# A planner that treats the ports shared by Vector and GpSimd as a lock, with offsets found anew

## The chip, the core and the metric

The kernel runs on one core of one Trainium2 chip. The time is device microseconds for one execution. A core has five engines that each work through a queue of their own in order: TensorE (PE in the profile, with its weight loads as PEld), VectorE (DVE), ScalarE (ACT), GpSimd (POOL) and SyncE (SP, which only starts DMAs here). They meet through semaphores alone.

## The reference, cut to what matters

```python
def reference(A_u, A_log_A_real, A_A_imag, A_C_real, A_C_imag, A_log_dt, A_D_skip, B_x, B_w_r, B_w_i, gate_w):
    x = A_u                                            # 1 x 2048 x 640
    g = _sigmoid((x * gate_w).sum(-1, keepdims=True))
    a = _A_ref(x, A_log_A_real, A_A_imag, A_C_real, A_C_imag, A_log_dt, A_D_skip)
    b = _B_ref(x, B_w_r, B_w_i)
    return g * a + (1 - g) * b

# _A_ref: K[d,l] = 2 Re sum_n C[d,n] exp(A[d,n] dt[d] l)   (640 x 128 states x 2048 positions)
#         y = irfft(rfft(u, 4096) * rfft(K, 4096))[:2048] + u * D_skip, per channel d
# _B_ref: irfft2(rfft2(x) * (w_r + 1j * w_i)) over positions and channels
```

## The kernel before, in words

All transforms are matrix products with tables. The work falls into streams, which the code names by a letter:

- **P** (`phase_p`): the preparation. Small elementwise chains on DVE and POOL turn `log_A_real`, `A_imag`, `C` and `log_dt` into eight rows of parameters. `parts` splits each into a rounded half and a rest, and writes it to the DRAM tile `par_d` by a DMA that POOL starts (L305).
- **A** (`phase_a`, first half): the forward transform of u in four chunks c of channels. Stage 1 (`p_s1`, L365) and stage 2 (`p_s2`, L378) run on PE; copies to `t1` and `ut` on ACT or DVE (L412); `ut` goes to DRAM as `u_d`. Between the halves of stage 1, gate products (`p_g`, L447) use the tile `z`, which POOL makes (L424); `z` has two buffers, so a new one waits for the gate product that read an old one.
- **B** (`phase_b`): the convolution kernel K in 40 tiles t, five at a time. Five tiles of magnitudes come first (PE `p_e` L665, ACT `e` L666), from parameters `par` that a DMA of POOL loads per five tiles (L656). Then each tile: PE `p_p` (L675), ACT and DVE `q` (L677, L678), DVE `aq` (L688), ACT `sc`, `sx`, `cx` (L690 to L693), DVE `x` (L700 to L702, against `sx` and `cx` in PSUM), POOL `y` (L705 and L706), and PE `p_k` (L719).
- **E** (`phase_a`, second half): the two-dimensional filter, in nine pairs of rows. DVE and POOL make `fo` and `fg` (L511 to L519), PE transposes and transforms, DVE multiplies (`mm`, `zz`, `pm`, L562 to L572) and combines (`xx`, `qq`).
- **D** (`phase_c`, `phase_d`): the products with the transform of K, the inverse and the gated sum. DVE makes `ma`, `mb` (from PSUM), `t2` and `oe`, POOL the other half of `t2` (L842) and the sum `ot` (L911).

The code's own order is only the input of a planner at its end. `steps` turns every instruction into a step with an engine, a length and the steps that it needs; `urgency` gives each a rank from its place in the code, the length of the work behind it, and the table `LEAD`; `arrange` walks through a modelled time and gives each engine the ready step of lowest rank; `keep_order` fixes the resulting order per engine. So a number in `LEAD` moves instructions on every engine. Before the change, the model lets DVE and POOL run side by side freely; for the preparation alone it stretches their lengths (`STRETCH`).

Of the kernel before, what the change touches and what calls it, by code (L numbers as in the profile page):

```python
# [15 lines left out]
PSUM = bass.MemoryType.PSUM  # L16
NOSYNC = mybir.DependencyInfo(mybir.DependencyClass.NoSync, mybir.DependencyReason.DATA)
DRAM = bass.MemoryType.DRAM

L = 2048  # L20
D = 640
N = 128
E = 321
# [778 lines left out]
def phase_d(tc, A, T, ctx, out):  # L802
# [174 lines left out]
RIGHT = ("a_", "f_", "c_t0", "c_k", "c_c", "c_u", "c_ps0")  # L977
SBUF_BYTES, PSUM_BYTES = 212992, 16384
DRAIN = {"PE": 0.1, "DVE": 0.083, "ACT": 0.115, "POOL": 0.045, "SP": 0.0}
STRETCH = {("P", "DVE"): 1.3, ("P", "POOL"): 1.15}  # L980
TABLES = {"Exp": "exp", "Sin": "sin", "Arctan": "sin", "Ln": "ln", "Sigmoid": "sig"}


LEAD = {
# [24 lines left out]
}  # L1009


def operands(ins, side):
    return [a for a in (getattr(o, "bass_ap", None) for o in getattr(ins, side)) if a is not None]
# [5 lines left out]

def on_chip(t):  # L1020
    return hasattr(t, "tag_meta") and "DRAM" not in str(t.space)


def pool_name(tag, pools):
# [8 lines left out]
def steps(traced):  # L1033

    insts = [x for x in traced if x.opcode != "TilePoolBoundary"]
# [3 lines left out]
    reads, writes = [[] for _ in insts], [[] for _ in insts]  # L1039
# [93 lines left out]
    for k, x in enumerate(insts):  # L1133
        e, name = ENGINES[str(x.engine).split(".")[-1]], short((writes[k] + reads[k])[0])
        if e == "PE":
            key = (writes[k][0], *(() if name == "p_s1" else (operands(x, "outs")[0].offset % 512 >= 160,) if name == "p_i2" else sorted(set(reads[k]))))
            if key in open_:
                home[k] = open_[key]
                todo[home[k]].parts.append(k)
                continue  # L1140
            open_[key] = len(todo)
        s = Step()
        s.engine, s.name, s.parts, s.dma = e, name, [k], x.opcode == "DMACopy"
        tag = [info[z].tag for z in writes[k] + reads[k] if on_chip(info[z])]
        pool = of[tag[0]] if tag else ""
        s.stream = "P" if pool in ("p1", "b_c") else "A" if pool == "cst" else {"b": "B", "a": "A", "f": "E"}.get(pool[:1], "D")
        s.table = TABLES.get(str(x.func).split(".")[-1]) if x.opcode == "Activation" else None
        s.first = reads[k]
        home[k] = len(todo)
        todo.append(s)  # L1150
    opened = {}
# [8 lines left out]
    for n, s in enumerate(todo):  # L1160
        s.needs = {home[j] for k in s.parts for j in needs[k]} - {n}
        s.behind = {home[j] for k in s.parts for j in turns[k]} - s.needs - {n}
        s.length = length(s, insts) * (1 if s.dma else STRETCH.get((s.stream, s.engine), 1))
        s.late = {"s3_d": 3.6, "t3": 4.0, "us": 3.0, "t3e": 3.0}.get(s.name, 3.4 if s.engine == "POOL" else 2.3)
        s.wire = 4 * math.prod(c for _, c in operands(insts[s.parts[0]], "outs")[0].ap) / (330e3 if s.name == "s3_d" else 390e3) if s.dma else 0
        if s.table in ("exp", "sin", "sig") and s.name in ("e", "sc", "sx", "cx", "gate"):
            s.needs |= {prior} - {None}
            prior = n
# [78 lines left out]
def arrange(todo, after, rank):  # L1247

    left = [len(s.needs | s.behind) for s in todo]
    come, start = [0.0] * len(todo), [0.0] * len(todo)  # L1250
    later = {e: [] for e in ENGINES.values()}
    ready = {e: [] for e in later}
    free = dict.fromkeys(later, 0.0)
    order = {e: [] for e in later}
    wire, table, end = 0.0, None, 0.0
    for n, c in enumerate(left):
        if not c:
            heapq.heappush(later[todo[n].engine], (0.0, n))
    for _ in todo:
        t, e = min((free[e] if ready[e] else max(free[e], later[e][0][0]), e) for e in later if ready[e] or later[e])  # L1260
        while later[e] and later[e][0][0] <= t:
            n = heapq.heappop(later[e])[1]
            heapq.heappush(ready[e], (rank[n], n))
        n = heapq.heappop(ready[e])[1]
        s = todo[n]
        start[n] = t
        own = t + s.length
        if s.table and s.table != table:
            own, table = own + 1.4, s.table
        free[e] = own  # L1270
        if s.dma:
            wire = max(wire, own) + s.wire
            own = wire + s.late
        elif e in ("DVE", "POOL"):
            own += DRAIN[e]
        seen = own + 0.05 + (DRAIN[e] if e in ("PE", "ACT") else 0)
        order[e].append(n)
        end = max(end, seen)
        for j in after[n]:
            if n in todo[j].needs:  # L1280
                come[j] = max(come[j], own if todo[j].engine == e else seen)
            left[j] -= 1
            if not left[j]:
                heapq.heappush(later[todo[j].engine], (come[j], j))
    return end, order, start
# [32 lines left out]
```

## Time and profile before

| | |
|---|---|
| time, median of 3 runs | 586.72 us (582.41 to 586.8) |
| the profiled execution | 585.55 us, span 582.6 us |
| busy PE, DVE, ACT, POOL | 512.2, 457.5, 359.0, 229.8 us |
| streams P, A, B and E | about 0 to 430 us, D from there to the end |

Busy time is the time in which an engine had an instruction of the program in work. An instruction that has been issued and stands still until something that it needs is free counts as busy, so a longer duration than that of its equals is a wait that no list of waits shows.

### The profile page before, as it was taken

To read this page: it belongs to the slowest core of one execution; us is meant where nothing else is said; L and a number is where in the kernel's file an instruction comes from. 1 tells how busy PE (TensorE), PEld (TensorE's weight loads), DVE (VectorE), ACT (ScalarE), POOL (GpSimd) and SP (SyncE) were. 2 spreads that over 40 slices of the span, in tenths; PEclk is the share of its full clock that TensorE was granted. 3 is DMA by queue.
4 is the path that set the end of the run, shared out by engine and by line. 5 is a ranking of instruction groups with operands and counts; after the bars stand their busy time and mean duration, and the time that the engine had idled before them with its cause. 6 is when DMAs were issued, how large, how long until landed. Compare 5 with 4: busy or idle time off the path is not lost. (4 is left out here: it accounts for less than half of the span.)

```text
span 582.6 us, 17664 instructions
## 1 busy us (share of the span) xinstructions
PE 512.2 (88%) x7580; PEld 382.5 (66%) x7580; DVE 457.5 (79%) x780; ACT 359.0 (62%) x655; POOL 229.8 (39%) x214
## 2 busy tenths in 40 slices
PE   2799899997888987999699999899879989999954
PEld 0798578766756756676567676666768767776621
DVE  4980369979988998998999998695956757677953
ACT  0665473567677976989778899688964333322110
POOL 3195033415432444443442451351632222635450
PEclk8899799998858998999999999699999999999997
DMA  9569415464051214124212122211849797999984
GB/s 344 193 233 357 148 47 201 157 188 168 25 169 58 75 50 136 56 68 147 114 57 69 55 70 78 92 52 46 318 167 335 239 349 282 311 324 344 346 266 174
DMA packets 47333, 100.64 MB, mean 173 GB/s; under 512 B 3204, under 2 KB 32280, under 8 KB 45368
## 3 DMA queue, kind: packets, MB, share of 16 engines
q1 hardware_dynamic: 25128, 69.35, 34.4%
q10 hardware_dynamic: 19088, 19.53, 10.1%
q0 software_dynamic: 3040, 10.65, 5.5%
q8 instruction: 59, 0.97, 0.6%
q14 instruction: 18, 0.15, 0.1%
HBM read 59.70 MB, written 39.81 MB: 171 GB/s over the span
## 5 line engine op out<-in xcount | busy, mean ns | idle before, releaser
L705 POOL TENSOR_TENSOR y<-e,sc 128x512 f32<-128x512 f32 x40 | 56.0, 1399 | 112.9 <-ACT sc L690 87.8
L378 PE MATMUL p_s<-t,w 128*64 128x160 f32 x1040 | 89.2, 312 | 2.1 <-ACT ut L412 2.0
L378 PEld LDWEIGHTS p_s<-t,w 128*64 128x64 f32 x1040 | 72.4, 137 | 19.8 <-issue 10.1
L666 ACT ACTIVATE e<-p_e 128x512 f32<-128x512 f32 x120 | 67.7, 612 | 20.4 <-PE p_e L665 19.5
L665 PE MATMUL p_e<-rm,par 128*128 128x512 f32 x120 | 57.4, 521 | 9.4 <-ACT e L666 6.1
L706 POOL TENSOR_TENSOR y<-e,sc 128x512 f32<-128x512 f32 x40 | 54.5, 1362 | 19.6 <-ACT sc L691 15.7
L678 DVE SCALAR_TENSOR_TENSOR q<-q,p_p 128x512 f32<-128x512 f32 x80 | 51.8, 676 | 12.8 <-ACT q L677 12.6
L842 POOL TENSOR_TENSOR t<-mb 128x320 f32<-128x320 f32 (+1 forms) x36 | 33.9, 943 | 70.3 <-DVE mb L840 64.8
L581 PE MATMUL p_eo<-td,pmt 107*128 107x321 f32 x204 | 58.8, 435 | 0.0
L366 ACT COPY t<-p_s 128x512 f32<-128x512 f32 x40 | 25.0, 634 | 54.3 <-PE p_s L365 43.6
L719 PE MATMUL p_k<-x,y 128*32 128x64 f32 x2560 | 45.2, 224 | 8.7 <-ACT kt L727 4.7
L675 PE MATMUL p_p<-rp,par 128*128 128x512 f32 x80 | 40.4, 534 | 14.0 <-DVE q L678 13.1
L365 PE MATMUL p_s<-c,u 128*64 128x128 f32 x640 | 40.0, 281 | 12.8 <-DMA u<-in_u_l 11.2
L719 PEld LDWEIGHTS p_k<-x,y 128*32 128x32 f32 x2560 | 39.1, 112 | 17.2 <-issue 10.7
L839 DVE TENSOR_TENSOR ma<-p_s,us 128x320 f32<-128x320 f32 (+1 forms) x68 | 32.9, 484 | 20.6 <-PE p_s L378 16.8
L702 DVE TENSOR_TENSOR x<-e,cx 128x1024 f32<-128x1024 f32 x40 | 48.3, 1208 | 0.6 <-ACT cx L693 0.6
L677 ACT ACTIVATE q<-p_p 128x512 f32<-128x512 f32 x80 | 44.9, 600 | 5.2 <-PE p_p L675 4.5
L581 PEld LDWEIGHTS p_eo<-td,pmt 107*128 107x128 f32 x204 | 38.2, 189 | 14.8
L365 PEld LDWEIGHTS p_s<-c,u 128*64 128x64 f32 x640 | 36.1, 140 | 17.9 <-DMA u<-in_u_l 12.8
L665 PEld LDWEIGHTS p_e<-rm,par 128*128 128x128 f32 x120 | 22.6, 201 | 29.5 <-ACT e L666 20.9
L365 PE MATMUL p_s<-c,kt 128*64 128x128 f32 x640 | 41.3, 274 | 0.1
L860 ACT COPY s<-p_i 128x640 f32<-128x640 f32 x32 | 20.6, 696 | 33.4 <-PE p_i L858 27.4
(152 smaller groups left out, 1093.4 us busy)
## 6 DMA issues: line engine op xcount, KB each, us to landing
u_d<-ut SPq DMA_DIRECT2D x32, 320.0 KB, 3.3
s_d<-s ACTq DMA_DIRECT2D x16, 640.0 KB, 5.8
t<-s_d SPq DMA_DIRECT2D x15, 640.0 KB, 6.5
us<-u_d ACTq DMA_DIRECT2D x13, 640.0 KB, 7.3
ww<-in_w_l SPq DMA_DIRECT2D x8, 642.0 KB, 3.9
ue<-u_d SPq DMA_DIRECT2D x8, 640.0 KB, 4.5
k_d<-kt SPq DMA_DIRECT2D x4, 1280.0 KB, 5.4
kt<-k_d SPq DMA_DIRECT2D x8, 640.0 KB, 6.2
```

The source lines that it names most:

```text
L365: nc.tensor.matmul(p[64 * ri:64 * ri + 64, j, :], src(i + j), e1[ri], start=True, stop=True)
L378: ins = nc.tensor.matmul(p[64 * j:64 * j + 64, i, 160 * ri:160 * ri + 160], w2[:, x, 64 * ri:64 * ri + 64], t1[:, x // 2 if x < 32 else K0 ...
L581: P.matmul(p[:, :E], st.pmt[:DC, c, w, j, :], tv[:DC, w, c, :], start=c == 0, stop=c == 2)
L665: P.matmul(p[:, :], pars[t], rm[:, c:c + 512], start=True, stop=True)
L666: S.activation(ef[:, c:c + 512], p[:, :], AF.Exp)
L675: P.matmul(p[:, :], pars[t], rp[:, c:c + 512], start=True, stop=True)
L677: S.activation(qf[:, c:c + 512], p[:, :], AF.Copy, bias=MAGIC)
L678: V.scalar_tensor_tensor(out=qf[:, c:c + 512], in0=qf[:, c:c + 512], scalar=MAGIC, in1=p[:, :], op0=ALU.subtract, op1=ALU.subtract)
L702: V.tensor_tensor(out=x[:, 0].rearrange("p d (h j) -> p d h j", h=2), in0=e[:, :, 0:64].rearrange("p d (h j) -> p d h j", h=2), in1=cx.uns ...
L705: G.tensor_tensor(out=y[:, 1], in0=e[:, :, 64:96], in1=sc[:, 0], op=ALU.mult)
L706: G.tensor_tensor(out=y[:, 0], in0=e[:, :, 64:96], in1=sc[:, 1], op=ALU.mult)
L719: P.matmul(st.pb[32 * r:32 * r + 32, o, :], y[:, ri, 4 * qq + JR[r], :], x[:, ri, 4 * qq + JR[r], :], start=t % 2 + qq + 1 - ri == 0, stop ...
```

## The change

The planner's time gets one variable more, `port`: the time at which the ports that DVE and POOL share become free. A step needs them (`s.port`) if POOL computes it, or if DVE runs it with all inputs in SBUF and either several inputs, or one input and an output in SBUF too. A step that needs the ports starts when they are free, and holds them until its end. Each engine's ready steps are kept in two heaps, without and with need of the ports; while the ports are taken, an engine takes a step without that need where it has one, whatever the ranks. DMAs that POOL starts are left out (`not s.dma`). `STRETCH` is dropped, and `LEAD` has the same keys with other numbers. What is computed, the buffers and the loops stay the same.

```diff
-STRETCH = {("P", "DVE"): 1.3, ("P", "POOL"): 1.15}
...
-    'mix': 0.53, 'A': (373, 290), 'B': (420, 624), 'D': (473, 238), 'E': (501, 524), 'P': (-536, -1704), ('A', 'DVE', 'ut'): -117,
+    'mix': 0.14, 'A': (279, 619), 'B': (522, 1248), 'D': (4113, 2809), 'E': (944, 678), 'P': (-1263, -2074), ('A', 'DVE', 'ut'): 143,
...
+def on_sbuf(ap):
+    return not any(w in str(ap.tensor.space) for w in ("PSUM", "DRAM"))
...
-        s.first = reads[k]
+        s.port = not s.dma and (e == "POOL" or e == "DVE" and all(on_sbuf(a) for a in operands(x, "ins")) and (
+            len(operands(x, "ins")) > 1 or x.opcode != "ScalarTensorTensor" and all(on_sbuf(a) for a in operands(x, "outs"))))
...
-        s.length = length(s, insts) * (1 if s.dma else STRETCH.get((s.stream, s.engine), 1))
+        s.length = length(s, insts)
...
-    ready = {e: [] for e in later}
+    ready = {e: ([], []) for e in later}
...
-    wire, table, end = 0.0, None, 0.0
+    wire, table, end, port = 0.0, None, 0.0, 0.0
...
-            heapq.heappush(ready[e], (rank[n], n))
-        n = heapq.heappop(ready[e])[1]
+            heapq.heappush(ready[e][todo[n].port], (rank[n], n))
+        a, b = ready[e]
+        n = heapq.heappop(a if a and (not b or b[0] > a[0] or port > t) else b)[1]
         s = todo[n]
+        if s.port:
+            t = max(t, port)
...
+        if s.port:
+            port = own + (DRAIN[e] if e == "POOL" else 0)
```

Three places show what this does to the rows.

DVE, at the products (`mm`, `zz`) of the third pair of rows of E, beside which it makes `fo` and `fg` for later pairs. Before:

```order
L702 TENSOR_TENSOR x<-e,cx 128x1024
L563 TENSOR_TENSOR mm<-xx,ww 128x642
L586 SCALAR_TENSOR_TENSOR qq<-o,c_65,p_eo 128x321
L587 SCALAR_TENSOR_TENSOR qq<-o,c_65,p_eo 128x319
L511 TENSOR_TENSOR fo<-ue 128x640
L512 TENSOR_TENSOR fo<-ue 128x640
L516 TENSOR_TENSOR fg<-fo 128x2x159
L564 TENSOR_TENSOR zz<-mm 128x321
L586 SCALAR_TENSOR_TENSOR qq<-o,c_65,p_eo 128x321
L587 SCALAR_TENSOR_TENSOR qq<-o,c_65,p_eo 128x319
L517 TENSOR_TENSOR fg<-fo 128x2x159
L565 TENSOR_TENSOR zz<-mm 128x321
```

The corresponding place after the change:

```order
L701 TENSOR_TENSOR x<-e,sx 128x16x32
L702 TENSOR_TENSOR x<-e,cx 128x1024
L516 TENSOR_TENSOR fg<-fo 128x2x159
L562 TENSOR_TENSOR mm<-xx,ww 128x642
L517 TENSOR_TENSOR fg<-fo 128x2x159
L563 TENSOR_TENSOR mm<-xx,ww 128x642
L564 TENSOR_TENSOR zz<-mm 128x321
L565 TENSOR_TENSOR zz<-mm 128x321
L511 TENSOR_TENSOR fo<-ue 128x640
L512 TENSOR_TENSOR fo<-ue 128x640
L566 TENSOR_TENSOR mm<-xx,ww 128x642
L567 TENSOR_TENSOR mm<-xx,ww 128x642
```

The steps with all inputs in SBUF (`fg`, `mm`, `zz`, `fo`) now stand together, and the `qq` and `x` steps, which read PSUM, ahead of them.

PE, where the magnitudes (`p_e`) and the first phases (`p_p`) of B begin between stage 1 and stage 2 of A's third chunk. Before:

```order
L365 MATMUL p_s_869<-c_65,u 64x128 x8
L665 MATMUL p_e<-rm,par 128x512 x2
L365 MATMUL p_s_889<-c_65,u 64x128 x8
L665 MATMUL p_e<-rm,par 128x512 x2
L447 MATMUL p_g<-u,z 32x64 x20
L675 MATMUL p_p<-rp,par 128x512 x2
L365 MATMUL p_s_947<-c_65,u 64x128 x8
```

After, from the group ahead of the last gate product to the first `p_p`:

```order
L365 MATMUL p_s_1087<-c_65,u 64x128 x8
L665 MATMUL p_e<-rm,par 128x512 x2
L447 MATMUL p_g<-u,z 32x64 x20
L665 MATMUL p_e<-rm,par 128x512 x2
L378 MATMUL p_s_1131<-t_816,w_68 64x160 x4
L665 MATMUL p_e<-rm,par 128x512
L378 MATMUL p_s_1137<-t_816,w_68 64x160 x4
L665 MATMUL p_e<-rm,par 128x512 x2
L378 MATMUL p_s_1193<-t_816,w_68 64x160 x4
L675 MATMUL p_p<-rp,par 128x512
```

The first `p_p` now stands behind five more stage 1 groups (947, 982, 1013, 1077, 1087), one more gate product and three stage 2 groups. None of the 15 `p_e` ahead of it comes before group 889 any more; 13 did.

POOL, at the end of the preparation, where `parts_203` is the last pair of parameter rows to be written to `par_d`. Before:

```order
L303 CAST parts_203<-th 128x640
L305 DMA par_d<-parts_176 128x1280
L304 TENSOR_TENSOR parts_203<-th,parts_203 128x640
L424 TENSOR_TENSOR z<-c_65,gw 128x640
L305 DMA par_d<-parts_203 128x1280
L424 TENSOR_TENSOR z<-c_65,gw 128x640 x2
L656 DMA par<-par_d 128x640 x2
```

After:

```order
L305 DMA par_d<-parts_191 128x1280
L303 CAST parts_203<-th 128x640
L424 TENSOR_TENSOR z<-c_65,gw 128x640
L304 TENSOR_TENSOR parts_203<-th,parts_203 128x640
L424 TENSOR_TENSOR z<-c_65,gw 128x640
L305 DMA par_d<-parts_203 128x1280
L656 DMA par<-par_d 128x640 x2
L424 TENSOR_TENSOR z<-c_65,gw 128x640 x2
```

Two of the `z` that stood behind the last write to `par_d` now stand ahead of it, the second of them the one that before waited for a gate product of chunk 1.

More of the change, by code (lines that the diff above doesn't have):

```diff
@@ L1259, in arrange @@
     for _ in todo:
-        t, e = min((free[e] if ready[e] else max(free[e], later[e][0][0]), e) for e in later if ready[e] or later[e])
+        t, e = min((free[e] if any(ready[e]) else max(free[e], later[e][0][0]), e) for e in later if any(ready[e]) or later[e])
         while later[e] and later[e][0][0] <= t:
             n = heapq.heappop(later[e])[1]
-            heapq.heappush(ready[e], (rank[n], n))
-        n = heapq.heappop(ready[e])[1]
+            heapq.heappush(ready[e][todo[n].port], (rank[n], n))
+        a, b = ready[e]
+        n = heapq.heappop(a if a and (not b or b[0] > a[0] or port > t) else b)[1]
         s = todo[n]
+        if s.port:
+            t = max(t, port)
         start[n] = t
```

47 rows, old and new, of the table LEAD are left out of this document.

## The prediction, made before the changed kernel ran

> **What bounds the kernel now.** I read the page's busy line first, then the busy time by stretch, then the chain that ended last.
>
> ```profile
> span 582.6 us, 17664 instructions
> PE 512.2 (88%) x7580; PEld 382.5 (66%) x7580; DVE 457.5 (79%) x780; ACT 359.0 (62%) x655; POOL 229.8 (39%) x214
> ```
>
> ```profile
> 60.00:80.00 20.00, 18.32 (x195) 12.87 (x197) 6.92 (x13) 10.67 (x19) 1.26 (x1) 0.83 0.28 92
> 80.00:100.00 20.00, 20.00 (x340) 16.59 (x338) 19.80 (x37) 11.25 (x19) 9.43 (x7) 1.00 0.41 153
> 60.00:430.00 370.00, 332.73 (x4508) 247.85 (x4508) 324.64 (x501) 288.48 (x533) 144.36 (x129) 0.94 0.32 107
> 180.00:330.00 150.00, 134.00 (x1570) 98.32 (x1572) 144.19 (x213) 124.26 (x233) 62.66 (x57) 0.97 0.27 85
> 330.00:430.00 100.00, 90.19 (x1310) 66.48 (x1299) 82.15 (x127) 87.22 (x167) 42.87 (x36) 0.95 0.32 109
> 480.00:540.00 60.00, 60.00 (x1032) 42.59 (x1028) 44.11 (x99) 18.17 (x29) 28.36 (x30) 1.00 0.91 315
> ```
>
> ```profile
> 430.22 0.64 issue
> ...
> 540.21 0.74 PE p_s L378 x8
> ```
>
> The columns after the stretch are busy us of PE, PEld, DVE, ACT and POOL, then granted clock, DMA share and GB/s. From 430 to 541 us the chain is matrix work back to back (PE 60.00 of 60): that is stream D. Ahead of it, streams A, B and E share all engines. Between 180 and 330 us DVE is the limit: 144.19 of 150 us, PE 134.00. Before and after, no engine is full (330 to 430: PE 90.19, ACT 87.22, DVE 82.15), so waits between engines set the pace.
>
> Part of DVE's busy time is no work. Here are neighbours on DVE and on POOL:
>
> ```profile
> 211.80 1.15 DVE L564 TENSOR_TENSOR zz<-mm 128x321 f32<-128x321 f32 x1
> 213.79 1.47 DVE L517 TENSOR_TENSOR fg<-fo 128x318 f32<-128x318 f32 x1
> ```
>
> ```profile
> 213.64 1.27 POOL L705 TENSOR_TENSOR y<-e,sc 128x512 f32<-128x512 f32 x1
> ```
>
> The fg step (0.48 us undisturbed, as L568 below, which has nearly its size) was issued at 213.79 while POOL's y ran until 214.91, and ended at 215.26: it began when y was done. That is the lock the new planner counts.
>
> **The change, part by part.** *The clashes.* The groups of DVE in 180 to 330 us, with mean ns after the busy us, and the spread of one line:
>
> ```profile
> L688 DVE TENSOR_SCALAR aq<-q 128x1024 int32<-128x1024 int32 x17 | 18.0, 1057 | 0.0
> L572 DVE TENSOR_TENSOR pm<-zz 128x642 f32<-128x642 f32 x5 | 5.8, 1162 | 0.0
> L571 DVE TENSOR_TENSOR pm<-zz 128x642 f32<-128x642 f32 x5 | 5.2, 1042 | 0.0
> L562 DVE TENSOR_TENSOR mm<-xx,ww 128x642 f32<-128x642 f32 x5 | 4.7, 936 | 0.0
> L567 DVE TENSOR_TENSOR mm<-xx,ww 128x642 f32<-128x642 f32 x5 | 4.1, 817 | 0.0
> L564 DVE TENSOR_TENSOR zz<-mm 128x321 f32<-128x321 f32 x5 | 3.7, 736 | 0.0
> L565 DVE TENSOR_TENSOR zz<-mm 128x321 f32<-128x321 f32 x5 | 3.5, 699 | 0.0
> L569 DVE TENSOR_TENSOR zz<-mm 128x321 f32<-128x321 f32 x5 | 3.1, 615 | 0.0
> L568 DVE TENSOR_TENSOR zz<-mm 128x321 f32<-128x321 f32 x5 | 2.4, 482 | 0.0
> L517 DVE TENSOR_TENSOR fg<-fo 128x318 f32<-128x318 f32 x5 | 3.4, 675 | 0.0
> L516 DVE TENSOR_TENSOR fg<-fo 128x318 f32<-128x318 f32 x5 | 3.1, 621 | 0.0
> ```
>
> ```profile
> L688 DVE TENSOR_SCALAR aq<-q x40: 674/683/2721, 81.7 to 422.2; 128x1024 int32<-128x1024 int32 x40
> ```
>
> Undisturbed, aq takes its median 683 ns, a 128x642 step 817 (L567), a 128x321 step 482 (L568). Lost: aq 17 x 374 = 6.4 us; pm and mm 5 x (345 + 225 + 119) = 3.4; zz 5 x (254 + 217 + 133) = 3.0; fg 5 x (193 + 139) = 1.7. Together **14.5 us**, in a stretch where DVE stands idle for only 5.8. All of it could reach the end: PE with 134.00 and ACT with 124.26 of 150 have room. What the new order saves lies between 0 (it fixes rows per engine, not when engines meet) and 14.5. The DVE excerpt shows both sides: zz, fo and mm were gathered behind the x products, which read PSUM, but fg on DVE still stands next to the fg that POOL makes from the same fo. Some aq are now followed by x, others by mm or zz, just where POOL starts y. I take half: **-7.3 us**. Outside the stretch DVE waits anyway (82.15 of 100 us from 330 on), so of what clashes cost there I count **-0.5 us**.
>
> *POOL's own DMA issues* stay outside the planner's lock.
>
> ```profile
> 286.13 0.61 POOL L656 DMA_DIRECT2D par<-par_d  x1
> ```
>
> ```profile
> 286.28 2.72 DVE L688 TENSOR_SCALAR aq<-q 128x1024 int32<-128x1024 int32 x1
> ```
>
> This aq stood 2.0 us beyond its 683 ns, behind an issue and the two fg that followed. Such clashes remain; that is a reason for half and not for all. The Trainium skill, SBUF — State Buffer (section "SBUF: two separate sides"), says that DMAs issued from GpSimd need the shared pair to write descriptors, so that a two-port Vector step and such an issue exclude each other, which the row at 286.28 fits. By that rule all 8 par issues can clash again, at 0.6 us each 4.8 us as an estimate; by the plan, none.
>
> *The start of B.* The preparation feeds par_d, whose last DMA now stands on POOL behind two z more, and the second of them waits for a gate product.
>
> ```profile
> 47.97 0.59 POOL L305 DMA_DIRECT2D par_d<-parts  x1
> 50.65 1.26 POOL L424 TENSOR_TENSOR z<-c,gw 128x640 f32<-128x640 f32 x1 [0.79 <-PE p_g L447]
> ```
>
> ```profile
> 61.68 1.19 PE L665 MATMUL p_e<-rm,par 128*128 128x512 f32 x2 [1.95 <-DMA par<-par_d]
> ```
>
> If that second z ends at 51.91 again, the DMA behind it goes out 3.9 us later than at 47.97, and the first p_e could run at 65.6 instead of 61.7. What covers it is work of A: the 13 p_e that stood ahead of p_s_889 now come behind it, so PE, free from 59.7, first does four and a half stage 2 groups and five of stage 1, 4.5 x 0.57 + 5 x 0.87 = 6.9 us (prices below), until 66.6. The cover is about 1 us thick; each us by which z waits longer than that is a us on the start of B. The move has its own price. Ahead of the first p_p stand five more stage 1 groups, one gate product and three stage 2 groups.
>
> ```profile
> 434.21 0.87 PE p_s L365 x16
> 435.09 1.14 PE p_s L378 x16
> ```
>
> ```profile
> 44.49 0.77 PE L447 MATMUL p_g<-u,z 128*32 128x64 f32 x40
> 79.26 1.29 DVE L678 SCALAR_TENSOR_TENSOR q<-q,p_p 128x512 f32<-128x512 f32 x2 [1.72 <-ACT q L677]
> L412 DVE COPY t<-p_s 128x512 f32<-128x512 f32 x20 | 13.2, 682 | 5.2 <-PE p_s L365 5.1
> L412 DVE COPY ut<-p_s 128x320 f32<-128x320 f32 x38 | 17.2, 481 | 25.5 <-DMA u_d<-ut 17.8 <-PE p_s L378 7.7
> ```
>
> A row of the order with x8 is 16 matmuls here, one with x4 is 8: 5 x 0.87 + 0.77 + 3 x 0.57 = 6.8 us, so DVE's first q comes at about 86 instead of 79.3. In return DVE has 5 t and 4 ut copies behind it by then, 5 x 0.68 + 4 x 0.48 = 5.3 us that it need not do later. Its net loss is **+1.5 us**, between -1 (PE has less to fill later) and +6.8 (the early copies only fill holes).
>
> *The rest.* In D, t2 and oe swap places with a neighbour and half of the inverse products stand together; PE's 60.00 of 60 us covers that: 0, or some 1 us if an evacuation comes late. The end (last s3 store, load and p_c) keeps its order. ACT loads as many tables. Without STRETCH the preparation steps only rank differently.
>
> Sum: -7.3 - 0.5 + 1.5 = **-6.3 us**. The profiled execution took 585.55 us (span 582.6 and 2.9 around it) and would take 579.3; it lies 1.2 us under the median of the runs, 586.72, which becomes **580.4**.
>
> **PE's clock** is the term that I can't set.
>
> ```profile
> 170.00:180.00 10.00, 9.04 (x31) 6.24 (x31) 6.59 (x12) 7.21 (x14) 2.19 (x3) 0.69 0.51 171
> 370.00:380.00 10.00, 10.00 (x97) 7.53 (x97) 3.86 (x8) 3.29 (x7) 2.59 (x2) 0.62 0.23 97
> ```
>
> ```profile
> PE p_p L675 <- DVE q L678: 13.1, 10, 3.2
> ```
>
> In these stretches the granted clock is 0.69 and 0.62, PE becomes the slow one, and DVE idles for 3.4 and 6.1 us. One such drop more or fewer is worth that much. PE's longest wait for q is 3.2 us; fewer clashes on DVE should shorten such waits, and waits at new places can bring a drop of their own. The Trainium skill, TensorE: Matmul & The Clock Gate (section "Part 1: The HAM clock gate"), halves the clock after an idle window of about 3.4 us and restores it after a busy one; by that rule waits of 3.2 us alone should cause no drop, and the sum would stand as it is. The rows show drops all the same, so here the trace does not agree; they decide, and the range takes a drop either way.
>
> **Rivals.**
> *Nothing reaches the end.* The order is by modelled times and the chip's waits drift against it; clashes move to other rows, as aq followed by mm. For: an order made without the lock already met only where the rows above show it, so there is chance in it. Against: DVE is full for 150 us. Then -0 + 1.5: about 588, and with a little saved 585.
> *All of it.* No clash stays in 180 to 330, and a steadier PE sees one clock drop fewer: 586.7 - 14.5 - 0.5 + 1.5 = 573, and 567 to 571 with that drop.
> *Slower, by the late start of B.* DVE lies two thirds idle before its first q (6.92 of 20 us); if that wait grows by all of 6.8 us because the copies moved ahead would have fitted into holes, and no clash is saved, the end comes at 586.7 + 6.8 = 593.5. It decides where savings stay under 1 us. For: between the first q and 180 us DVE has some holes (6.59 of 10 from 170 on). Against: 80 to 100 us has next to none (19.80 of 20).
>
> **How the numbers follow.** The forecast (577 to 584) has 0.38, no effect (584 to 592) 0.26, all of it (under 577) 0.18, slower (over 592.6) 0.18. One per cent, 5.9 us, is about what a measurement here tells from no change. Below 580.9 lie all of the third case and 0.26 of the forecast's own range: faster 0.44; same 0.12 + 0.26 = 0.38; slower 0.18. The range 570 to 593 leaves out the deepest savings with a clock drop fewer and the worst of the late start.
>
> **What would show it.** Clashes: between 180 and 330 us mean aq near 0.87 us instead of 1.06, pm near 0.96 instead of 1.10. Bound: DVE near 448 us in total, PE's share of the span higher. Start: first q near 86 us, par landing before PE asks for it. D: about 152 us from its start to the end, as now. I am wrong if aq stays over 1.0, if the first q comes after 90, or if the count of stretches with a halved clock changes by two.

## The result, and the profile after

The changed kernel takes **579.66 us** (median of 8 runs, 577.0 to 581.85), the kernel before on the same chips 585.41 us (8 runs, 582.41 to 588.19). The ratio is **0.9894**, with a 95% interval of 0.9859 to 0.9928. The forecast was 580.4. The profiled execution took 580.48 us. Ratios are of means, and runs over 1.5% above the fastest of their kernel are left out of them.

The page of the changed kernel, its span and busy line:

```profile
span 578.5 us, 17670 instructions
PE 505.8 (87%) x7580; PEld 380.9 (66%) x7580; DVE 453.1 (78%) x780; ACT 356.7 (62%) x655; POOL 226.9 (39%) x214
```

Its busy time by stretch, with the columns of the prediction:

```profile
60.00:430.00 370.00, 329.75 (x4682) 248.27 (x4680) 323.07 (x505) 287.58 (x537) 142.57 (x129) 0.97 0.33 109
180.00:330.00 150.00, 134.06 (x1631) 99.43 (x1629) 143.76 (x220) 124.54 (x236) 63.02 (x59) 0.99 0.27 83
330.00:430.00 100.00, 88.30 (x1400) 66.11 (x1402) 77.86 (x121) 84.07 (x161) 39.90 (x34) 0.97 0.32 112
```

DVE is still full between 180 and 330 us (143.76 of 150). Busy time went down a little on DVE (457.5 to 453.1) and POOL (229.8 to 226.9), and no instruction was taken out: what fell there is standing still. (PE's fall, 512.2 to 505.8, also holds its higher clock.) The groups of DVE in 180 to 330 us (busy us, mean ns):

```profile
L688 DVE TENSOR_SCALAR aq<-q 128x1024 int32<-128x1024 int32 x18 | 15.8, 880 | 0.0
L566 DVE TENSOR_TENSOR mm<-xx,ww 128x642 f32<-128x642 f32 x5 | 6.0, 1205 | 0.0
L567 DVE TENSOR_TENSOR mm<-xx,ww 128x642 f32<-128x642 f32 x5 | 5.2, 1031 | 0.0
L571 DVE TENSOR_TENSOR pm<-zz 128x642 f32<-128x642 f32 x5 | 5.1, 1012 | 0.1
L572 DVE TENSOR_TENSOR pm<-zz 128x642 f32<-128x642 f32 x5 | 5.0, 992 | 0.0
L565 DVE TENSOR_TENSOR zz<-mm 128x321 f32<-128x321 f32 x5 | 3.1, 623 | 0.0
```

The clash of DVE with POOL, worked out as in the prediction (count times mean over the undisturbed length), is 3.5 us for aq (18 x 197 ns), 3.7 for mm, 1.9 for pm, 0.8 for zz and 0.7 for fg: 10.6 us, where it was 14.5. aq, pm, zz and fg lost less; mm, which now meets POOL's y (an mm at 232.61 us took 1.89 us beside a y issued at 232.54), lost 3 us more.

Two landmarks cut the program into parts: the 40 aq mark stream B, the first ma the start of D. The duration column is lowest, median and highest ns, then come the first and the last start. In the changed kernel, and in it alone the fifth aq:

```profile
L688 DVE TENSOR_SCALAR aq<-q x40: 675/682/1912, 86.6 to 416.8; 128x1024 int32<-128x1024 int32 x40
L839 DVE TENSOR_TENSOR ma<-p_s,us x68: 474/481/492, 428.5 to 551.3; 128x320 f32<-128x320 f32 x64, 32x320 f32<-32x320 f32 x4
```

```profile
109.58 0.68 DVE L688 TENSOR_SCALAR aq<-q 128x1024 int32<-128x1024 int32 x1
```

In the kernel before:

```profile
111.95 0.68 DVE L688 TENSOR_SCALAR aq<-q 128x1024 int32<-128x1024 int32 x1
L839 DVE TENSOR_TENSOR ma<-p_s,us x68: 476/481/492, 433.8 to 556.0; 128x320 f32<-128x320 f32 x64, 32x320 f32<-32x320 f32 x4
```

B starts 4.9 us later (81.7 to 86.6), but is 2.4 us ahead at its fifth tile, 5.4 ahead at its last (422.2 to 416.8), and D begins 5.3 us earlier. From the first ma to the end of the span D takes 148.8 us before and 150.0 after, so 4.1 us are left of 5.3. The lead at the fifth aq is one of time, not of work: the new order has put some copies and x steps behind it (counted below). All this is against the first profile of the kernel before; a second one, further down, has a span of 578.9 us, only 0.4 above the changed kernel's.

### The profile page after: what moved, and what is told of

Its sections match the earlier page's. It is cut to its first block, busy times and chain, and to the rows that moved or that the text cites. A ratio compares the mean times of both kernels' runs of the same rounds, so it can differ in the third digit from the quotient of the medians.

```text
span 578.5 us, 17670 instructions
## 1 busy us (share of the span) xinstructions
PE 505.8 (87%) x7580; PEld 380.9 (66%) x7580; DVE 453.1 (78%) x780; ACT 356.7 (62%) x655; POOL 226.9 (39%) x214
## 5 line engine op out<-in xcount | busy, mean ns | idle before, releaser
L665 PE MATMUL p_e<-rm,par 128*128 128x512 f32 x120 | 53.8, 492 | 12.0 <-DVE q L678 5.9
L719 PE MATMUL p_k<-x,y 128*32 128x64 f32 x2560 | 47.2, 225 | 6.9 <-DVE x L702 3.4
L365 PE MATMUL p_s<-c,u 128*64 128x128 f32 x640 | 41.7, 287 | 11.9 <-DMA u<-in_u_l 11.1
L675 PE MATMUL p_p<-rp,par 128*128 128x512 f32 x80 | 38.8, 509 | 11.5 <-DVE q L678 10.2
L365 PEld LDWEIGHTS p_s<-c,u 128*64 128x64 f32 x640 | 37.8, 145 | 16.2 <-DMA u<-in_u_l 12.5
L412 DVE COPY ut<-p_s 128x320 f32<-128x320 f32 (+1 forms) x41 | 19.1, 484 | 33.1 <-ACT ut L412 21.4
L365 PEld LDWEIGHTS p_s<-c,kt 128*64 128x64 f32 x640 | 36.4, 136 | 9.8 <-issue 7.2
```

The costliest lines, as they stand in the source:

```text
L365: nc.tensor.matmul(p[64 * ri:64 * ri + 64, j, :], src(i + j), e1[ri], start=True, stop=True)
L665: P.matmul(p[:, :], pars[t], rm[:, c:c + 512], start=True, stop=True)
L675: P.matmul(p[:, :], pars[t], rp[:, c:c + 512], start=True, stop=True)
L719: P.matmul(st.pb[32 * r:32 * r + 32, o, :], y[:, ri, 4 * qq + JR[r], :], x[:, ri, 4 * qq + JR[r], :], start=t % 2 + qq + 1 - ri == 0, stop ...
```

## The experiments

**Theory 1**: time is lost where DVE and POOL want the shared ports at once, and the rule that keeps them apart in the plan saves it. **Theory 2**: the rule by itself brings nothing; the offsets found anew pace the streams better. Ratios below are against the kernel before on the same chip, with 95% intervals.

### The rule without the offsets, and the offsets without the rule

The changed kernel with the old `LEAD` (`lock_old`; like the changed kernel, it has no `STRETCH`):

```diff
-    'mix': 0.14, 'A': (279, 619), 'B': (522, 1248), 'D': (4113, 2809), ...
+    'mix': 0.53, 'A': (373, 290), 'B': (420, 624), 'D': (473, 238), ...
```

> The new planner (lock, no STRETCH) with the offsets of before. Theory 1, the lock pays by itself: 1 to 3 us under the kernel before, and the time that DVE loses to clashes between 180 and 330 us falls from 14.5 us to 11 or less. Theory 2, the offsets pay: the time stays within 3 us of before or rises, since these offsets were found for another planner, whatever the clashes do.

The changed kernel with the new `LEAD` and no step that needs the ports (`new_nolock`, without `STRETCH` too):

```diff
-        s.port = not s.dma and (e == "POOL" or e == "DVE" and all(on_sbuf(a) ...
+        s.port = False
```

> The new offsets with the lock rule off (no step needs the ports). Theory 1: the gain is lost, 584 to 588 us, and clashes on DVE between 180 and 330 us are back at 14 us or more. Theory 2: most of the gain stays, 578 to 582 us, with clashes at 14 us or more.

Measured: the rule with the old offsets 0.9975 [0.9929, 1.0021], no clear difference; the new offsets without the rule **1.0494** [1.0421, 1.0566], far slower. Its busy time by stretch:

```profile
180.00:330.00 150.00, 129.63 (x1472) 95.97 (x1472) 144.34 (x210) 111.67 (x211) 58.67 (x53) 0.97 0.29 92
330.00:430.00 100.00, 91.84 (x1167) 65.18 (x1167) 69.47 (x104) 81.57 (x157) 32.90 (x30) 0.93 0.28 98
```

DVE is as busy as ever up to 330 us, with 210 instructions done instead of 220, and starved after. Its clashes are 16.7 us. Neither half brings the gain alone, so both theories are wrong as stated: the offsets fit only the rule with which they were found. (What dropping `STRETCH` does by itself was not tried.)

But the rule did its part: with the old offsets the clashes in 180 to 330 us are 5.8 us, fewer than the 10.6 of the changed kernel. What was saved there must have been given back elsewhere.

### Less for the two to fight over

POOL's two products y, of e and sc, become copies of sc (`ycopy_before` in the old order, `ycopy_after` in the new). The product with e is left out of the computation; the order of instructions is the same in each case.

```diff
-        G.tensor_tensor(out=y[:, 1], in0=e[:, :, 64:96], in1=sc[:, 0], op=ALU.mult)
+        G.tensor_copy(y[:, 1], sc[:, 0])
```

> The kernel before, in the same order, but POOL makes y by copying the sine tiles instead of multiplying them by the magnitudes (that product is left out), so POOL holds the ports for about half as long per y. Theory 1: clashes are what DVE loses, so the 14.5 us fall to about 7 and the time by 4 to 7 us, to 579 to 582. Theory 2: clashes fall as much, but the time by less than 2 us, since waits between engines take it back.

> The changed kernel with the same replacement for y (the product with the magnitudes is left out), in the same order. Its clashes between 180 and 330 us, about 10.7 us, should fall by half too. Theory 1: 3 to 5 us under the changed kernel, to 575 to 577. Theory 2: within 2 us of it.

Measured: 0.9754 [0.9679, 0.9829] in the order before and 0.9752 [0.9629, 0.9875] in the new order. y, some 1.4 us in both orders, now holds the ports half as long (the order before, 180 to 330 us, and its busy time there):

```profile
L705 POOL COPY y<-sc 128x512 f32<-128x512 f32 x20 | 15.8, 790 | 62.9 <-ACT sc L690 50.9 <-PE p_k L719 6.3 <-ACT pmt L535 3.9
L688 DVE TENSOR_SCALAR aq<-q 128x1024 int32<-128x1024 int32 x19 | 14.2, 745 | 0.0
180.00:330.00 150.00, 141.27 (x1783) 105.00 (x1782) 143.91 (x230) 132.71 (x253) 46.64 (x65) 0.99 0.29 87
```

DVE does 230 instructions in the stretch where it did 213, in the same busy time, and PE follows (134.00 to 141.27 us). The clashes fall to 3.9 and 5.4 us. The order before gains 2.5%, some 14 us, about twice the most that was expected of it; the changed kernel gains some 1.4% on top of its 1.1%, and the two end alike, as they would if the advantage of the new order were there only while POOL holds the ports long. That is for the clashes as the lever, but doesn't show it: the intervals, 0.8 and 1.2% to each side, are as wide as the advantage itself, and a shorter y also feeds p_k sooner.

### Where the old offsets gave it back

With the rule and the old offsets the last aq stood at 412.6 us, 9.6 ahead of the kernel before, yet the first ma at 432.1: the hand-over from B to D took 19.5 us instead of 11.6. ACT had a copy t of D ahead of the last tile's sc. So D's start offset alone was set to its new value, once with the rule (`lock_D`) and once in the kernel before (`before_D`):

```diff
-    ... 'D': (473, 238), ...
+    ... 'D': (4113, 238), ...
```

> The new planner with the old offsets, and of these one pair changed: stream D's start offset 473 becomes 4113, its new value, so that D's first copies stand behind the last steps of B (five rows move on PE, six on ACT, none on DVE or POOL). With the old offsets the last aq came at 412.6 us and the first ma 19.5 us later, against 11.6 before: ACT held the last tile's sc behind a t copy of D, which waited for the load of kt. Theory 1 (the rule saves time where DVE and POOL meet, and the old offsets gave 8 us of it back at the hand-over to D): about 574 us, 8 less than the 582 of the new planner with the old offsets, and under the changed kernel's 579.7. Theory 2 (the offsets found anew pace B and E, and the rule by itself brings nothing): the hand-over was only the end of work that is late anyway; 580 to 583.

> The kernel before with the same pair alone: D's start offset 4113 for 473, and no lock. Theory 1: the hand-over costs only what PE waits there, 1.9 us for kt and 2.4 us for y; a gain of 0 to 4 us, 581 to 585 beside the 585 of before, and at least 7 us over the kernel that has the lock as well. Theory 2 (the change's gain comes from such offsets): 579 to 580, the whole gain of the change without any lock.

Measured: `lock_D` 1.0033 [1.0, 1.0067], no gain at all; `before_D` 0.9964 [0.993, 0.9998], 2 us, as theory 1 expected of it, but faster than with the rule, where theory 1 wanted it 7 us slower. The theory of the copy on ACT fell: with the copy out of the way the hand-over still took 19.8 us (last aq 414.0, first ma 433.8). On PE, with the rule and D's offset, stands this (the time in brackets is idle time before the row, and what ended it):

```profile
411.44 1.92 PE L719 MATMUL p_k<-x,y 128*32 128x64 f32 x121
417.93 0.33 PE L719 MATMUL p_k<-x,y 128*32 128x64 f32 x4 [4.57 <-issue]
```

PE stood for 4.57 us within one group of 128 products and waited for nothing that the profile shows ("issue"). Before it went on the granted clock was halved, for 6.8 us from 417.0:

```profile
417.10:423.80 6.70, 5.87 (x69) 5.52 (x72) 2.42 (x3) 5.25 (x10) 2.50 (x2) 0.50 0.83 327
```

The five profiles with a hand-over of 19 to 20 us (`lock_old`, `lock_D`, `lock_D_w3`, `lock_D_mix`, `lock_D_dma_mix`) all have this pause, of 4.5 to 4.6 us, and 6.8 us of halved clock that begin within it; the other nine have no "issue" wait over 2.7 us. An estimate from these rows: in `lock_D` the pause and half of the 5.9 us of halved clock behind it come to 7.5 us, and its hand-over is 8.2 us longer than that of the kernel before.

From 410.4 us on D's first loads filled the DMA engines, and in 405 to 420 us the queue that brings instructions moved one packet:

```profile
q8 instruction: 1, 0.02, 0.4%
```

By the trace it ran at 415.4 us, 5 us after the loads began, and PE went on 1.5 us after its end. The reading that PE waited for instructions whose fetch stood behind the loads was tried by starting the last of them, w3, later, from ACT (`lock_D_w3`):

```diff
-    nc.sync.dma_start(T.w3[:, :, :, :], ...
+    nc.scalar.dma_start(T.w3[:, :, :, :], ...
-    ('D', 'SP', 'w3'): -663
+    ('D', 'ACT', 'w3'): 200
```

> The new planner with the old offsets and D's start at 4113, with one thing moved: the 1088 KB load of w3 for stream D is started by ACT behind the last but one cx, some 2.5 us later, and not by SP behind the us loads. No other row moves. In the kernel without this, PE stood for 4.57 us at 413.4 to 417.9 in the middle of a p_k product with nothing that it waited for, while D's first loads ran at over 400 GB/s from 410.4 and one 16 KB packet of the instruction queue ran at 415.4. Theory 1 (PE waits for its next instructions, whose fetch stands behind those loads): the wait shrinks to 2.5 us or less, and the end comes 2 to 4 us earlier, 582 to 584. Theory 2 (the pause has another cause, the loads only stand beside it): it stays at 4 to 5 us, and the time at 586.

Measured: 1.0028 [0.9994, 1.0062], and the pause stayed:

```profile
418.79 0.33 PE L719 MATMUL p_k<-x,y 128*32 128x64 f32 x4 [4.54 <-issue]
```

w3's first packet ran at 416.9 us there, the instruction packet at 416.5, ahead of it. So the expectation was wrong, and the run speaks against w3 as the cause, but not against kt and us, which were still loaded first. That PE waits for instructions is borne out by the other traces: all 14 together have 20 such waits of PE over 1.2 us, and in each PE went on 1.1 to 1.5 us after a packet of the instruction queue had ended. A whole run has only some 92 of these packets, so this is no chance. What holds the packet back at the hand-over **stays open**: waits of 1.5 us stand where the DMA engines were idle as well (at 378 us in `lock_old`), and delaying kt and us, which would tell, was not tried.

The other place is the start. In `lock_D` the first aq comes at 87.2 us, against 81.7. DVE and POOL in its preparation:

```profile
41.46 5.58 DVE L304 TENSOR_TENSOR parts<-q,parts 128x640 fp32r<-128x640 f32 x1
```

```profile
41.02 0.65 POOL L305 DMA_DIRECT2D par_d<-parts  x1
41.71 1.58 POOL L304 TENSOR_TENSOR parts<-lar,parts 128x640 fp32r<-128x640 f32 x1
43.24 1.27 POOL L424 TENSOR_TENSOR z<-c,gw 128x640 f32<-128x640 f32 x1
44.45 0.60 POOL L305 DMA_DIRECT2D par_d<-parts  x1
45.06 1.28 POOL L424 TENSOR_TENSOR z<-c,gw 128x640 f32<-128x640 f32 x1
```

The DVE step takes 0.81 us by itself (its like at 37.6 us). Issued at 41.46 while POOL issued a DMA, it ended at 47.04, 0.7 us after the second z: it stood 4.8 us behind four more instructions of POOL, and got in only when POOL had none left. But this clash isn't what makes B late. In `lock_D_dma` (next section), where B starts 5.8 us earlier, the same step ends later, at 48.29:

```profile
46.17 2.12 DVE L304 TENSOR_TENSOR parts<-q,parts 128x640 fp32r<-128x640 f32 x1
```

What differs is the first gate product. POOL makes its z only at 25.96 us in `lock_D` (at 23.31 in `lock_D_dma`, at 9.78 in the kernel before), and PE waits for it, here in `lock_D` and then in `lock_D_dma`:

```profile
27.44 0.94 PE L447 MATMUL p_g<-u,z 128*32 128x64 f32 x40 [4.22 <-POOL z L424]
24.86 0.77 PE L447 MATMUL p_g<-u,z 128*32 128x64 f32 x40 [1.52 <-POOL z L424]
```

In `lock_D` the clock is halved for 3.4 us behind that wait. The later gate products, the z that wait for them and the last write to par_d (57.97 us against 52.48) are then 5.5 us late, and so is B.

### POOL's DMAs under the rule

The plan lets POOL's DMA issues run beside DVE. In `lock_D_dma` they hold the ports too:

```diff
-        s.port = not s.dma and (e == "POOL" or e == "DVE" and ...
+        s.port = (e == "POOL" or e == "DVE" and ...
```

> The new planner with the old offsets and D's start at 4113, and the DMAs that POOL starts hold the ports in the model too, for the length of their issue. Theory 1 (clashes cost time wherever they are; 8 par issues and the s3e_d issues meet DVE's steps at up to 2 us for an aq): 2 to 4 us less than the same kernel without this, unless the order it gives loses them elsewhere; no aq longer than 1.6 us. Theory 2: no difference beyond that of any new order, plus or minus 5 us either way.

Measured: **574.1 us, 0.9834** [0.9791, 0.9877], against 1.0033 without that edit: 12 us where 2 to 4 were expected, and the lowest time here of a kernel that computes everything. Its interval overlaps the changed kernel's by a little. The first aq is back at 81.4 us, and the hand-over is 8.8 us:

```profile
L688 DVE TENSOR_SCALAR aq<-q x40: 677/686/1770, 81.4 to 412.5; 128x1024 int32<-128x1024 int32 x40
L839 DVE TENSOR_TENSOR ma<-p_s,us x68: 475/482/493, 421.3 to 544.1; 128x320 f32<-128x320 f32 x64, 32x320 f32<-32x320 f32 x4
```

The longest aq, 1.77 us, is over the 1.6 expected: what is left of clashes is 6.0 us between 180 and 330 us, no less than the 5.9 of `lock_D`. By the last aq this kernel is only 1.5 us ahead of `lock_D`; another 11 us come at the hand-over, where the pause of 4.6 us is missing. The edit moves rows on every engine (by line and tile, 171 of DVE's 780 instructions), so is it the rule, or one lucky order? The offset `mix` was set from .53 to .54, with and without it:

> The fastest kernel so far (new planner, old offsets, D's start at 4113, POOL's DMA issues hold the ports too; 574.1 us) with the offset mix .54 for .53, which moves some 340 rows on PE and 260 on DVE. Theory 1 (the rule for POOL's DMAs saves the time, whatever the order): 571 to 579, and at least 5 us under the same mix without that rule. Theory 2 (574.1 was one lucky order among many): about as the same mix without that rule, 580 to 588.

> The same mix .54 in the new planner with the old offsets and D's start at 4113, without the rule for POOL's DMAs (586.1 us at mix .53). Theory 1: 580 to 588, at least 5 us over the same mix with that rule. Theory 2: anything between 572 and 590, the spread that any new order has.

Measured: 0.9979 [0.9934, 1.0025] with the DMAs under the rule, 1.0103 [1.0046, 1.0159] without. The edit is worth 2.0% in the first pair and 1.2% in the second, intervals apart in both. But the level moved by over 1% in `lock_D_dma_mix`, so 571 to 579 was wrong, and some of the 574.1 belongs to that one order. The two pairs aren't independent either: without the rule for DMAs, .54 gives nearly the order of .53 (11 of DVE's 780 instructions stand elsewhere). The second pair is the closer test, with 56 of 780 moved: its hand-overs are alike, the last aq comes 6.6 us earlier, and the medians are 6.9 us apart, as theory 1 said. Its clashes between 180 and 330 us don't fall, though (8.7 against 7.3), so how the edit gains there isn't shown. For the order of the changed kernel itself the same was asked (`after_mix`, `mix` .20 for .14):

> The changed kernel with the offset mix .20 for .14, which moves some 310 rows on PE and 260 on DVE; the rule and all other offsets are as changed. Theory 1 (the rule by itself sets the time): within 4 us of 579.7. Theory 2 (the offsets were found for this one order, and any other order under the same rule gives it up): 585 to 600.

Measured: 1.0067 [1.0016, 1.0117] (median of all 12 runs 592.4 us), with clashes of 9.8 us, as few as in the changed kernel: another order under the same rule and with one offset changed loses the gain and more.

### The kernel before again

> The kernel before once more, unchanged, for a second profile of the same order at another granted clock (the first was 582.6 us at 0.941; its other runs went from 578.7 at 0.961 to 587.7 at 0.936). Theory 1 (clashes set the time): the mean aq between 180 and 330 us stays near 1.06 us and moves with the span; theory 2 (the clock sets it, whatever the clashes): at a higher clock the span is shorter by about 2.6 us per 0.01 with the same clashes, the same excess of DVE (27 us over its undisturbed lengths).

Its second profile, of the same instructions in the same order:

```profile
core 0: 578.9 us, clock 0.947
```

```profile
L688 DVE TENSOR_SCALAR aq<-q 128x1024 int32<-128x1024 int32 x18 | 17.6, 977 | 0.0
```

It is 3.7 us shorter than the first. Clashes are 12.0 us instead of 14.5, the clock higher by 0.006: both theories foretold some of it, and it doesn't divide them. It bounds what one pair of profiles can tell: terms of 2 to 3 us are within what one order does from execution to execution.

All profiles side by side (us; clashes worked out as above, in 180 to 330 us):

| kernel | clashes | first aq | last aq | first ma | span | ratio |
|---|---|---|---|---|---|---|
| before | 14.5 | 81.7 | 422.2 | 433.8 | 582.6 | 1 |
| before, second profile | 12.0 | 82.6 | 418.9 | 430.5 | 578.9 | |
| changed | 10.6 | 86.6 | 416.8 | 428.5 | 578.5 | 0.9894 |
| `before_D` | 13.2 | 81.6 | 421.5 | 431.2 | 579.2 | 0.9964 |
| `new_nolock` | 16.7 | 73.1 | 451.6 | 458.8 | 609.2 | 1.0494 |
| `after_mix` | 9.8 | 85.9 | 428.6 | 436.5 | 584.1 | 1.0067 |
| `lock_old` | 5.8 | 87.4 | 412.6 | 432.1 | 582.0 | 0.9975 |
| `lock_D` | 5.9 | 87.2 | 414.0 | 433.8 | 584.9 | 1.0033 |
| `lock_D_w3` | 5.7 | 89.5 | 414.9 | 434.7 | 585.1 | 1.0028 |
| `lock_D_mix` | 7.3 | 86.6 | 415.8 | 435.4 | 585.8 | 1.0103 |
| `lock_D_dma` | 6.0 | 81.4 | 412.5 | 421.3 | 571.2 | 0.9834 |
| `lock_D_dma_mix` | 8.7 | 84.2 | 409.2 | 429.1 | 579.8 | 0.9979 |
| `ycopy_before` | 3.9 | 83.5 | 408.0 | 421.1 | 570.1 | 0.9754 |
| `ycopy_after` | 5.4 | 85.7 | 407.5 | 420.5 | 570.9 | 0.9752 |

Every row with under 10 us of clashes has its last aq 6 to 15 us ahead of the first profile of the kernel before, but for `after_mix`, which lost its lead after 330 us. Whether the end follows is decided at the hand-over to D: 7 to 13 us from the last aq to the first ma in some orders, 19 to 20 in others (the five with the pause), whatever the clashes. The changed kernel removes fewer clashes than its rule can, and its hand-over (11.7 us) gives none of it back.

## Why the prediction was right, point by point

The time was right and the mechanism was at work, but one term of the sum was half of what was forecast, and a gain that no term foresaw stood in for the rest: the closeness of the total is partly luck.

- **Clashes, forecast -7.3 us.** Mis-sized: 3.9 us less than in the first profile of before, 1.4 less than in the second. Of the named signs aq came (0.880 us, 0.87 forecast), pm nearly (1.00, 0.96), and DVE's total half (453.1, 448). "Half" was taken from one look at which rows stand together; what zz and fg saved, 3.1 us, mm lost at its new place.
- **POOL's own DMA issues.** Right. The same clash as at 286.28 us stands in the changed kernel:

```profile
284.39 0.61 POOL L656 DMA_DIRECT2D par<-par_d  x1 [0.81 <-PE p_p L675]
284.54 1.91 DVE L688 TENSOR_SCALAR aq<-q 128x1024 int32<-128x1024 int32 x1
285.02 0.87 POOL L517 TENSOR_TENSOR fg<-fo 128x318 f32<-128x318 f32 x1
```

  The rule of the Trainium skill, SBUF — State Buffer (section "SBUF: two separate sides"), that such an issue and a two-port Vector step exclude each other, fits this row. The prediction's estimate of 4.8 us for all 8 was a bound; the pairs of runs put 1.2% and 2.0% on the edit, with what else it moves.
- **The start of B, forecast +1.5 us.** Its path was right: z waits for a gate product, the last par_d issue comes 3.5 us later, PE doesn't wait for par, the first q comes at 84.94 us (86 forecast):

```profile
50.26 1.26 POOL L424 TENSOR_TENSOR z<-c,gw 128x640 f32<-128x640 f32 x1 [1.51 <-PE p_g L447]
51.46 0.60 POOL L305 DMA_DIRECT2D par_d<-parts  x1
```

  Its size was about right, though the landmark hides it. By its fifth aq the new order is 2.4 us ahead (3.3 against the second profile), but there DVE has done three t copies (0.68 us each) and three x steps (two of 0.67, one of 1.20) fewer: 4.6 us of work. In work it is 2.2 us behind, 1.3 by the second profile. No PE wait for par is left, which cost 2.0 us before.
- **Outside the stretch, forecast -0.5 us.** Here a term is missing: the waits between the start of B and 180 us were put at nothing. Before, then after:

```profile
112.00:180.00 68.00, 58.21 (x834) 43.39 (x835) 59.66 (x97) 49.99 (x88) 24.76 (x25) 0.85 0.43 143
112.00:180.00 68.00, 58.81 (x896) 44.64 (x893) 63.43 (x102) 53.86 (x97) 26.24 (x26) 0.92 0.48 158
```

  DVE works 3.8 us more there (1.7 more than in the second profile, at a clock of 0.90), with about as much lost to clashes (some 4.2 us over the undisturbed lengths in both): it waits less, and PE's clock is halved for 10 us there instead of 20. Which of the two brings the other isn't shown.
- **D, 0 to +1 us.** 1.2 us, about as bounded (1.6 against the second profile).
- **The end.** The parts close: 2.2 us behind at the start, 3.8 and 3.9 gained, make 5.5, and the last aq is 5.4 ahead; D takes 1.2 of it, and the profiles show -4.1. Against the second profile the same sum gives 1.8, the last aq is 2.1 ahead, and the spans differ by 0.4. The forecast's -6.3 us and the 5.8 between the medians agree because the clash term was 3.4 us too large and the missing gain, 3.8 against the first profile, about as large.
- **PE's clock, left open.** The clock over 60 to 430 us went from 0.94 (0.95 in the second profile) to 0.97. At half speed for the rest, that is 0.06 x 370 / 0.5 = 44 us of halved clock, then 22. The count of such stretches, which was to prove me wrong if it changed by two, is 6, 8 and 6 in the three profiles: it isn't even fixed for one order, and was no test. In the three sets of runs of the kernel before (12, 23 and 23), the time fell by 2.6, 1.9 and 1.7 us for each 0.01 of mean clock, and the changed kernel's runs average 0.963 against 0.944 to 0.947: by that some 3 to 4 of the 5.8 us go with the clock. In the first profile of before and in the changed kernel's, waits of PE of 1.5 to 3.2 us stand ahead of every drop from 59 to 430 us but one (at 394.2 us in the changed kernel), so this need not be a cause apart from the waits and clashes, and no run here separates them.
- **Rivals.** "Slower by the late start" failed, since the start cost some 2 us and not 6.8. "All of it" failed, since 10.6 us of clashes stayed. "Nothing reaches the end" describes the rule with the old offsets (0.9975), not the change; the mechanism named for it, waits that drift against the plan, was there as the hand-over.

## What to carry to other kernels

Count the clashes from the group means, then follow landmarks through the program: a stream that ended 9.6 us earlier handed 7.9 of it back at the next border between streams (`lock_old`). At each landmark, count the work behind it too: a step that comes earlier may only have passed others. A planner's rule and the offsets searched under it are one change; tested apart, either can lose. And in a plan that treats an engine pair as exclusive, let the DMAs that the pair issues count as well: that was 2.0% and 1.2% faster here, though not by fewer clashes where these were counted.

## What the runs showed of the hardware

- A DVE step that needs the shared ports can get in between two instructions of POOL: the fg issued at 213.79 us in the kernel before ended at 215.26, and POOL's next y, issued in between, took 1.52 us instead of 1.27:

```profile
214.88 1.52 POOL L706 TENSOR_TENSOR y<-e,sc 128x512 f32<-128x512 f32 x1
```

  The longest waits shown here (41.46 us in `lock_D`, 286.28 before, 284.54 in the changed kernel) were issued while POOL issued a DMA, and those steps came only behind the computing instructions that followed, 4.8 us behind four instructions at the worst. The price of a clash can be the length of POOL's run; what decides which it is isn't shown.
- PE can stand for 4.5 us within a group of matrix products, waiting for nothing that the profile shows, while loads fill the DMA engines (in five profiles), and goes on 1.1 to 1.5 us after a packet of the instruction queue. In the changed kernel such waits come to 5.5 us (us in total, times, the longest), in the first profile of the kernel before to none:

```profile
PE p_s L365 <- issue: 3.7, 2, 2.2
PE p_k L719 <- issue: 1.8, 3, 0.8
```

  They may be part of what the changed kernel still gives back.
- PE's clock was halved in the changed kernel from 138.2 to 145.0 us, after a wait of 2.36 us for q and with PE busy for only 1.64 of the 4 us ahead, and stayed halved with PE busy:

```profile
134.00:138.00 4.00, 1.64 (x74) 1.24 (x73) 3.94 (x7) 2.53 (x5) 3.31 (x2) 1.00 0.35 91
138.20:145.00 6.80, 5.97 (x21) 5.00 (x22) 6.76 (x12) 5.14 (x10) 3.41 (x3) 0.50 0.64 219
```

  The Trainium skill, TensorE: Matmul & The Clock Gate (section "Part 1: The HAM clock gate"), asks in its table for an idle window of about 3.4 us; a wait of 2.36 us in a thinly used stretch was enough here, so if idle means without any product, the trace does not agree.
